# VectorE's order around a shared PSUM bank in a Winograd feed-forward kernel: the sum that frees bank b goes ahead of the residue, and two softmax steps go a place later

## The chip, the cores and the metric

The kernel runs on one core of one Trainium2 chip. The metric is the device time of one launch in microseconds (us), median of several runs. TensorE (PE in the profile, its weight loads PEld), VectorE (DVE), ScalarE (ACT), GpSimd (POOL) and SyncE (SP) each work through a queue of their own, in the order in which the program issues to them; semaphores between the queues keep the data right.

## The reference

Channel attention over four batches, then a feed-forward layer with an ELU over all tokens.

```python
B, N, C = (4, 6080, 256)            # q, k, v
n_tokens, d_model, d_ff = (24320, 256, 2048)
...
qn = q / (np.linalg.norm(q, axis=1, keepdims=True) + 1e-06)
kn = k / (np.linalg.norm(k, axis=1, keepdims=True) + 1e-06)
s = kn.transpose(0, 2, 1) @ qn / tau
s = s - s.max(-1, keepdims=True)
a = np.exp(s)
a /= a.sum(-1, keepdims=True) + 1e-09
x = (v @ a)                          # 256 channels a token
h = x @ w_in
g = np.where(h > 0.0, h, np.exp(np.minimum(h, 0.0)) - 1.0)
return g @ w_out
```

## The kernel before, in words

**Precision and folding.** Each float32 operand of a large product is split in a high part, rounded to the matmul's input format, and a low part, the residue (operand minus its high part). A product is then three matmuls: high by high, high by low, low by high. The softmaxed matrix `a` of a batch is multiplied into `w_in` once, so that a token's hidden values come straight from `v`.

**Units.** The tokens of batches 1 to 3 go through 36 chunks of 512 or 496 tokens, and each chunk through four quarters of the 2048 hidden features (`fq`). A chunk and a quarter make a unit, 144 in all (lines 1471 to 1537). Within a unit the product of a 2 by 2 block matrix with a 2 by 2 block matrix is done by Winograd's scheme, with seven block products in place of eight: A11·B11, S3·T3, S2·T2, A12·B21, S1·T1, S4·B22 and A22·T4, where the S and T are sums of blocks. Their partial sums are put together in three PSUM banks, `bank_a`, `bank_b` and `bank_e`, of which `bank_b` is one and the same for all units. `product` (line 1104) is six matmuls.

**Bank b in a unit.** ScalarE copies A11·B11 from `bank_a` into `bank_b` (line 1490) and S3·T3 from `bank_e` into `p` (`vp`, line 1492). TensorE adds S2·T2 on top in `bank_b`. VectorE then makes the sum `ve = vb + vp` (line 1500), which reads `bank_b`; only then may TensorE go on to add S1·T1 in `bank_b`. VectorE makes `vp = vb + vp` (line 1506) of that; only then may TensorE add S4·B22. So TensorE waits for VectorE at the start of S1·T1 and of S4·B22, and for ScalarE (line 1490) at the start of S2·T2.

**ELU and residues.** For each of the four blocks of hidden values ScalarE makes Relu (line 1183) and Exp (line 1184) into a buffer `held` or `other`, and VectorE combines them with the block (`largest`, line 1187). The block for row 0, half 0 is called e11 in the code, and is the first of a unit; the next is e22, then e12 and e21. Then the high part of g is made by a DMA that GpSimd issues (line 1204), for e12 by ScalarE (line 1202). The low part, g's residue, is `lo_parts` (line 1212, or two instructions of line 1210 when the row's blocks lie in `other`): it reads the block and the high part that the DMA wrote. The residue of row 0 of unit u is made in unit u+1 behind S2·T2, that of row 1 behind `largest` of e11. Row 0's blocks lie in `held[:, 0]`, which the next unit's Relu of e11 writes over, so that Relu waits until row 0's residue has been made.

**Second layer.** Between the block products stand the matmuls of the second layer, three to an item (lines 1127, 1128 and 1129, the last with g's residue as its operand), eight items a unit, two at a time (`multiply_out`). The items of row 0 of unit u begin behind S1·T1 of unit u+1.

**What sets the order.** The instructions of a unit are issued in the order of the code. Between them stand calls of `spend(engine, budget, now)`: each takes tasks from lists (loads, splits, the next batches' attention) whose inputs are far enough back, and issues them there. `now` counts quarters of a unit. A task on another engine's result is ready when that result was issued `late` places earlier; without `late`, VectorE's tasks may be issued in the same place as ScalarE's task they read (`GAP[DVE]` is 0, line 951). While units run, the attention of batches 2 and 3 is made in such tasks. The softmax part is in `plan_soft`: ScalarE takes a square root of the norms and loads the table for Exp (lines 1384 and 1386), VectorE turns this into inverse norms (lines 1391 to 1406: a guard, two halves of a reciprocal, three refining steps, again two halves of a reciprocal), scales the rows (1420 to 1422), ScalarE takes Exp with row sums (1427), VectorE inverts these sums (`over_sums`, lines 318 and 319).

Of the kernel before, what the change touches and what calls it, by code (L numbers as in the profile page):

```python
# [27 lines left out]
def in_turns(cols):  # L28

    if len(cols.shape) == 3:  # L30
        return cols.rearrange("p x (a b) -> p x b a", a=2)
    return cols.rearrange("p (a b) -> p b a", a=2)
# [22 lines left out]
def channel_attention_then_elu_ffn(ctx: ExitStack, tc, q, k, vT, tau, w_in, w_out, outT):  # L55
# [8 lines left out]
    nc = tc.nc  # L64
# [252 lines left out]
    def over_sums(sm):  # L317
        nc.vector.tensor_scalar(sm, sm, 1e-9, None, op0=ALU.add)
        nc.vector.reciprocal(sm, sm)
# [233 lines left out]
    state = {}  # L553
# [395 lines left out]
    ACT, DVE, POOL, PE, SP = "act", "dve", "pool", "pe", "sp"  # L949
# [18 lines left out]
    def task(engine, cost, fn, deps=(), when=0, level=1, late=None):  # L968

        t = Task(fn, tuple(d for d in deps if d is not None), when)  # L970
        t.late, t.engine = late, engine
        t.cost = cost
        queues[engine, level].append(t)
        return t

    def spend(engine, budget, now):
        for level in range(-2, 4):
            queue = queues[engine, level]
            while True:
                able = [t for t in (queue if level < 2 else queue[:1]) if t.ready(now)]  # L980
                if not able or able[0].cost > budget + 0.3:
                    break
                t = able[0]
                queue.remove(t)
                budget -= t.cost
                t.fn()
                t.done = now
# [30 lines left out]
    def half_of(c):  # L1018
        return span(c)[2] // 2
# [47 lines left out]
    x = s1 - 13  # L1067
# [29 lines left out]
    def product(bank, c, fq, a, t, begin=False):  # L1097
        hn = half_of(c)
        w, m = s_tiles[fq][:, :, MATRICES.index(a)], operands[c, t]
        hi, lo = (in_turns(m[:, x, 0:hn]) for x in range(2))  # L1100
        for j in range(2):
            js = slice(j * P, j * P + P)
            for k, (x, y) in enumerate(((0, hi), (0, lo), (1, hi))):
                nc.tensor.matmul(  # L1104
                    bank[:, j, 0:hn],
                    w[:, x, js],
                    y,
                    start=(begin and j == 0 and k == 0),
                    stop=(j == 1 and k == 2),
                    skip_group_check=True,  # L1110
                )
# [44 lines left out]
    def multiply_out(count, now):  # L1156
        for _ in range(count):
            if not outs:
                return
            item = outs.pop(0)  # L1160
            if item is None:
                continue
            for _ in out_matmuls(*item):
                beside(now)
# [30 lines left out]
    def exact(u, row, half, hn):  # L1195
        e = others[half] if row == 1 and u % 2 == 1 else held[:, row, half]
        return e[:, 0 : 2 * hn]
# [17 lines left out]
    def plan_chunk(c):  # L1215

        if c + 1 >= NCH:
            return
        d, t = c + 1, begins[c]
        if c == NB:  # L1220
            task(SP, 0, lambda: new_t_group(d), when=t, level=0)
        x = task(SP, 0, lambda: vraw.__setitem__(d, load_v(d)), when=t + PERIOD, level=0)
        for k in range(3):
            x = task(DVE, 0.415 if k else 0.685, lambda k=k: t_sum(d, k), [x], when=t + PERIOD, level=0)
            if k != 1:
                y = task(ACT, 0.61, lambda k=k: t_hi(d, k), [x], when=t + PERIOD, level=0, late=1)
                task(DVE, 0.685, lambda k=k: t_lo(d, k), [y], when=t + PERIOD, level=-1, late=1)
        for k, when in enumerate((2 * PERIOD, 3 * PERIOD, 3 * PERIOD + 1)):
            y = task(POOL, 0.55, lambda k=k: b_hi(d, k), when=t + when, level=0)
            task(DVE, 0.415, lambda k=k: b_lo(d, k), [y, x], level=-2, late=2)  # L1230
# [106 lines left out]
    def plan_soft(b, t):  # L1337
# [20 lines left out]
        def row_copy(ct):  # L1358
            if ct == 0:
                state[b, "a"] = work.tile([P, KT, C], F32, tag="a", bufs=1, name=f"a_{b}")  # L1360
            nc.scalar.copy(halves(state[b, "a"][:, ct]), halves_of_turns(state[b, "gram"][ct][:, 1, :]))
# [6 lines left out]
        for ct in range(KT):  # L1368
            x = task(ACT, 0.35, lambda ct=ct: row_copy(ct), [last_gram], level=0)
# [18 lines left out]
        x = task(ACT, 1.0, root, [pn], level=0)  # L1388
# [22 lines left out]
        turns = [[(0.95, lambda half=half, of=of: turned(half, of)) for half in range(2)] for of in ("ry", "y")]  # L1411
        refining = [(cost, lambda k=k: refined(k)) for k, cost in enumerate((0.42, 0.42, 0.3))]
        for cost, fn in ((0.3, guarded), *turns[0], *refining, *turns[1], (0.2, taken)):
            x = task(DVE, cost, fn, [x], level=0)

        def scaled(ct, k):
            a = state[b, "a"]
            row = halves(a[:, ct])
            (
                lambda: nc.vector.tensor_scalar(a[:, ct], a[:, ct], n["rk"][:, ct : ct + 1], None, op0=ALU.mult),  # L1420
                lambda: nc.vector.tensor_mul(row, row, n["rq"]),
                lambda: nc.vector.tensor_reduce(n["nm"][:, ct : ct + 1], a[:, ct], axis=AX.X, op=ALU.max, negate=True),
            )[k]()

        def exped(ct):
            a = state[b, "a"]
            nc.scalar.activation(
                a[:, ct], a[:, ct], AF.Exp, bias=n["nm"][:, ct : ct + 1], accum_out=state[b, "rs"][:, ct : ct + 1]
            )

        exps = []
        for ct in range(KT):
            for k, cost in enumerate((0.25, 0.42, 0.42)):
                x = task(DVE, cost, lambda ct=ct, k=k: scaled(ct, k), [x], level=0)
            exps.append(task(ACT, 0.5, lambda ct=ct: exped(ct), [x], level=0))
        sums = task(DVE, 0.2, lambda: over_sums(state[b, "rs"]), exps, level=0)

        def transposes():
            n["pt"] = ps.tile([P, KT, C], F32, tag="gram", bufs=KT, name="pt")
# [16 lines left out]
        x = task(ACT, 0.61, aT_hi, [pt, folded], level=0)  # L1456
        x = task(DVE, 0.685, aT_lo, [x], level=0)
# [13 lines left out]
    for u, (c, fq) in enumerate(units):  # L1471
        now = PERIOD * u
        b = c // NB
        hn = half_of(c)
        if fq == 0:
            plan_chunk(c)
        spend(SP, 1, now)
        assert (b, fq) in s_ready, (b, fq, u)
        e11, e12, e21, e22 = (
            exact(u, row, half, hn).rearrange("p (j t) -> p j t", j=2) for row in range(2) for half in range(2)  # L1480
        )
        vp = p7[:, :, 0:hn]
        bank_a = ps.tile([P, 2, HF], F32, tag="w", bufs=WB, name="bank_a")
        bank_e = ps.tile([P, 2, HF], F32, tag="w", bufs=WB, name="bank_e")
        va, vb, ve = (bank[:, :, 0:hn] for bank in (bank_a, bank_b, bank_e))

        product(bank_a, c, fq, "A11", "B11", True)
        if before is not None:
            before[0]()
        nc.scalar.copy(vb, va)  # L1490
        product(bank_e, c, fq, "S3", "T3", True)
        nc.scalar.copy(vp, ve)
        multiply_out(2, now)
        spend(POOL, 3.9, now)
        spend(ACT, 2.0, now)
        spend(DVE, 2.4 if u % (FQ * NB) in (0, *range(FQ * NB - FQ, FQ * NB)) else 1.7, now)
        product(bank_b, c, fq, "S2", "T2")
        if before is not None:
            before[1]()
        nc.vector.tensor_add(ve, vb, vp)  # L1500
        product(bank_a, c, fq, "A12", "B21")
        relu_exp(e11, va)
        multiply_out(2, now)
        spend(ACT, 0.7, now + 1)
        product(bank_b, c, fq, "S1", "T1")
        nc.vector.tensor_add(vp, vb, vp)  # L1506
        multiply_out(2, now + 1)
        largest(e11, va)
        hi_part(u, 0, 0, hn)
        spend(POOL, 1.2, now + 1)  # L1510
        product(bank_b, c, fq, "S4", "B22")
        product(bank_e, c, fq, "A22", "T4")
        if before is not None:
            before[2]()
        relu_exp(e22, vp)
        largest(e22, vp)
        hi_part(u, 1, 1, hn)
        relu_exp(e12, vb)
        relu_exp(e21, ve)
        largest(e12, vb)  # L1520
        hi_part(u, 0, 1, hn, True)
        multiply_out(2, now + 2)
        spend(DVE, 1.4, now + 2)
        spend(ACT, 0.4, now + 2)
        spend(POOL, 3.3, now + 2)
        spend(SP, 1, now + 2)

        def finish(e21=e21, ve=ve, u=u, hn=hn):
            largest(e21, ve)
            hi_part(u, 1, 0, hn)  # L1530

        before = (finish, lambda u=u, hn=hn: lo_parts(u, 0, hn), lambda u=u, hn=hn: lo_parts(u, 1, hn))

        for y, row in ((2, 0), (0, 1)):
            for dt in range(DT):
                for j in range(2):
                    outs.append((c, 4 * fq + y + j, ((u, row), j), dt))
# [46 lines left out]
```

## Time and profile before

| | |
|---|---|
| median of 3 runs | 2140.25 us (2137.35 to 2141.48) |
| the profiled execution's own time | 2139.17 us |
| its span, first to last instruction | 2137.4 us |
| granted TensorE clock, mean | 1.000 |
| units | 144, from about 597 us to the end |

A row of a timeline gives the start in us from the span's start, the duration, the engine, the line, the operation, what it writes and reads by the program's names, its shape and how often; in brackets the idle time of that engine just before it and what ended that. A row of a wait table gives who waited for whom, the total in us, how often, and the longest. Matmuls overlap (a new one starts before the last one's end), so an engine with a busy share of 99% may still lose time to waits.

### The profile page before, as it was taken

What the parts mean: (1) busy time and instruction counts of PE and PEld (TensorE: products, weight loads), DVE (VectorE), ACT (ScalarE), POOL (GpSimd) and SP (SyncE); (2) the same over time, 40 slices, a digit from 0 to 9 for tenths busy, and PEclk for the clock granted to TensorE, in tenths of its full rate; (3) what the DMA queues carried; (4) which work ended last, traced back from release to release, by engine and by line L of the source; (5) the groups of instructions that cost most, each with busy time, mean ns of one, the idle gap of its engine ahead of it and who ended that gap; (6) DMA issues with size and microseconds to landing.
All of it is one profiled execution on the core that took longest, in us unless ns stands there. A gap on an engine that the chain in (4) does not pass through costs nothing. (4 is left out here: it accounts for less than half of the span.)

```text
span 2137.4 us, 34932 instructions
## 1 busy us (share of the span) xinstructions
PE 2108.5 (99%) x12833; PEld 1930.5 (90%) x12833; DVE 1584.1 (74%) x2380; ACT 1485.0 (69%) x2524; POOL 439.2 (21%) x763
## 2 busy tenths in 40 slices
PE   9999999999999999999999999999999999999999
PEld 8888888899889998999899899999899999999998
DVE  7987777777777777777677777777767777776775
ACT  6877777767766776667666677667766676776765
POOL 0000000000233333321233333322133222121121
PEclk9999999999999999999999999999999999999999
DMA  9320221210357887854366778875436443333432
GB/s 361 109 79 30 72 79 64 74 56 30 133 162 215 220 221 206 224 161 133 115 188 208 201 216 217 229 202 162 130 121 188 128 124 116 113 122 111 127 99 94
DMA packets 163371, 312.27 MB, mean 146 GB/s; under 512 B 17408, under 2 KB 59520, under 8 KB 161664
## 3 DMA queue, kind: packets, MB, share of 16 engines
q0 software_dynamic: 101376, 191.00, 32.7%
q1 hardware_dynamic: 61680, 118.91, 16.2%
q8 instruction: 102, 1.67, 0.3%
q14 instruction: 69, 0.57, 0.1%
q10 hardware_dynamic: 144, 0.13, 0.0%
HBM read 134.33 MB, written 31.20 MB: 77 GB/s over the span
## 5 line engine op out<-in xcount | busy, mean ns | idle before, releaser
L1127 PE MATMUL po<-g,wo 128*128 128x512 f32 (+1 forms) x1158 | 438.9, 379 | 0.0
L1129 PE MATMUL po<-g,wo 128*128 128x512 f32 (+1 forms) x1158 | 437.1, 377 | 0.0
L1128 PE MATMUL po<-g,wo 128*128 128x512 f32 (+1 forms) x1158 | 436.9, 377 | 0.0
L1204 POOL DMA_DIRECT2D g<-held x288 | 154.1, 535 | 926.7 <-DVE held L1187 589.6
L1212 DVE TENSOR_TENSOR g<-held,g 128x1024 fp32r<-128x1024 f32 (+1 forms) x216 | 263.8, 1221 | 34.2 <-DMA g<-held 33.2
L1184 ACT ACTIVATE held<-held 128x512 f32<-128x512 f32 (+1 forms) x432 | 270.4, 626 | 13.8
L1104 PEld LDWEIGHTS bank_b<-t,s 128*128 128x128 f32 x1728 | 232.7, 191 | 48.8 <-DVE bank_e L1500 28.2
L1506 DVE TENSOR_TENSOR p<-bank_b,p 128x512 f32<-128x512 f32 (+1 forms) x144 | 98.8, 686 | 238.8 <-PE bank_b L1104 238.8
L1104 PE MATMUL bank_b<-t,s 128*128 128x256 f32 (+1 forms) x1728 | 243.2, 277 | 21.7 <-DVE bank_e L1500 15.2
L1129 PEld LDWEIGHTS po<-g,wo 128*128 128x128 f32 x1158 | 218.9, 189 | 28.3
L1104 PE MATMUL bank_e<-t,s 128*128 128x256 f32 (+1 forms) x1728 | 240.0, 275 | 0.0
L1128 PEld LDWEIGHTS po<-g,wo 128*128 128x128 f32 x1158 | 220.2, 190 | 17.2
L1127 PEld LDWEIGHTS po<-g,wo 128*128 128x128 f32 x1158 | 220.7, 191 | 13.1
L1183 ACT ACTIVATE held<-bank_a 128x512 f32<-128x512 f32 (+1 forms) x144 | 85.2, 592 | 189.6 <-PE bank_a L1104 128.9
L1104 PEld LDWEIGHTS bank_e<-t,s 128*128 128x128 f32 x1728 | 216.1, 192 | 0.0
L1104 PE MATMUL bank_a<-s,s 128*128 128x256 f32 (+1 forms) x1296 | 179.8, 275 | 0.0
L1104 PEld LDWEIGHTS bank_a<-s,s 128*128 128x128 f32 x1296 | 168.4, 192 | 4.7
L115 DVE TENSOR_TENSOR g<-e,g 128x512 fp32r<-128x512 f32 (+1 forms) x192 | 131.7, 686 | 48.6 <-ACT g L114 47.2
L114 ACT CAST g<-e 128x512 fp32r<-128x512 f32 (+1 forms) x192 | 116.7, 608 | 70.7 <-DVE e L447 38.7
L474 PE MATMUL po<-g,wo 128*128 128x512 f32 (+1 forms) x378 | 142.7, 377 | 0.0
L472 PE MATMUL po<-g,wo 128*128 128x512 f32 (+1 forms) x378 | 142.6, 377 | 0.0
L470 PE MATMUL po<-g,wo 128*128 128x512 f32 (+1 forms) x378 | 142.6, 377 | 0.0
(228 smaller groups left out, 4333.4 us busy)
## 6 DMA issues: line engine op xcount, KB each, us to landing
g<-held POOLq DMA_DIRECT2D x192, 256.0 KB, 3.0
g<-other POOLq DMA_DIRECT2D x96, 256.0 KB, 3.3
g<-held POOLq DMA_DIRECT2D x96, 248.0 KB, 2.2
acc<-sq POOLq DMA_DIRECT2D x46, 512.0 KB, 5.1
raw<-in_q_dram SPq DMA_DIRECT2D x76, 256.0 KB, 4.2
raw<-in_k_dram SPq DMA_DIRECT2D x76, 256.0 KB, 4.7
v<-in_v_dram SPq DMA_DIRECT2D x32, 512.0 KB, 5.6
out_dram<-o SPq DMA_DIRECT2D x56, 256.0 KB, 2.1
```

What stands on the lines that cost most here:

```text
L114: nc.scalar.copy(hi, src)
L115: nc.vector.tensor_sub(lo, src, hi.bitcast(F32))
L470: nc.tensor.matmul(o, wo[:, f, 0, ds], hi, start=first(c, f), stop=False)
L472: nc.tensor.matmul(o, wo[:, f, 1, ds], hi, start=False, stop=False)
L474: nc.tensor.matmul(o, wo[:, f, 0, ds], lo, start=False, stop=last(c, f))
L1104: nc.tensor.matmul(bank[:, j, 0:hn], w[:, x, js], y, start=(begin and j == 0 and k == 0), stop=(j == 1 and k == 2), skip_group_check=True,)
L1127: yield nc.tensor.matmul(o, wo[:, f, 0, ds], hi, start=begin, stop=False)
L1128: yield nc.tensor.matmul(o, wo[:, f, 1, ds], hi, start=False, stop=False)
L1129: yield nc.tensor.matmul(o, wo[:, f, 0, ds], lo, start=False, stop=end)
L1184: nc.scalar.activation(e, e, AF.Exp, scale=-1.0)
L1204: nc.gpsimd.dma_start(to, e)
L1212: nc.vector.tensor_sub(lo, held[:, row, :, 0 : 2 * hn], hi.bitcast(F32))
```

## The change

Two edits. In the unit, `before[1]()`, which is the residue of row 0 of the unit before, and the sum `ve = vb + vp` change places on VectorE: the sum is issued first. In `plan_soft`, the steps of the inverse norms and the inversion of the row sums get `late=1`: they may not be issued in the same place as ScalarE's result, but one place later; the second is also entered with a cost of 0.35 in place of 0.2.

```diff
         for cost, fn in ((0.3, guarded), *turns[0], *refining, *turns[1], (0.2, taken)):
-            x = task(DVE, cost, fn, [x], level=0)
+            x = task(DVE, cost, fn, [x], level=0, late=1)
...
-        sums = task(DVE, 0.2, lambda: over_sums(state[b, "rs"]), exps, level=0)
+        sums = task(DVE, 0.35, lambda: over_sums(state[b, "rs"]), exps, level=0, late=1)
...
         product(bank_b, c, fq, "S2", "T2")
+        nc.vector.tensor_add(ve, vb, vp)
         if before is not None:
             before[1]()
-        nc.vector.tensor_add(ve, vb, vp)
         product(bank_a, c, fq, "A12", "B21")
         relu_exp(e11, va)
```

The order of instructions changes on VectorE alone; TensorE, ScalarE, GpSimd and SyncE keep theirs. The sum is line 1500 before and line 1498 after.

VectorE in the unit in which the softmax of batch 2 begins (the 36th; batch 3 has the same rows 48 units later), before: the last steps of the unit before it, the guard and a half reciprocal, the residue of row 0, the sum, the second sum.

```order
L1187 SCALAR_TENSOR_TENSOR held<-held,bank_e 128x496
L1040 TENSOR_TENSOR t_5096<-tt_8744,t_5096 128x2x248
L1391 TENSOR_SCALAR ry<-y 128x260
L1395 RECIPROCAL ry<-ry 128x130
L1212 TENSOR_TENSOR g_5223<-held,g_5162 128x2x496
L1500 TENSOR_TENSOR bank_e<-bank_b,p_5094 128x2x248
L1506 TENSOR_TENSOR p_5094<-bank_b,p_5094 128x2x248
```

The same place after, and what follows up to the guard:

```order
L1187 SCALAR_TENSOR_TENSOR held<-held,bank_e 128x496
L1040 TENSOR_TENSOR t_5096<-tt_8744,t_5096 128x2x248
L1498 TENSOR_TENSOR bank_e<-bank_b,p_5094 128x2x248
L1212 TENSOR_TENSOR g_5224<-held,g_5162 128x2x496
L1506 TENSOR_TENSOR p_5094<-bank_b,p_5094 128x2x248
L1187 SCALAR_TENSOR_TENSOR held<-held,bank_a 128x496
L1212 TENSOR_TENSOR g_5224<-held,g_5162 128x2x496
L1187 SCALAR_TENSOR_TENSOR other_5093<-other_5093,p_5094 128x496
L1187 SCALAR_TENSOR_TENSOR held<-held,bank_b 128x496
L1062 TENSOR_TENSOR s_4777<-v_8709,s_4777 128x248
L1391 TENSOR_SCALAR ry<-y 128x260
L1395 RECIPROCAL ry<-ry 128x130
```

The sum stands ahead of the residue, here as in each of the 143 units that have a residue to make; the guard and the first half reciprocal have moved behind three blocks' `largest`. The later steps of the chain move too: the unit after this one makes one half reciprocal more, and two refining steps move from it into the one after that. From there on the chain has its old places.

VectorE at the end of the softmax, before: the last block of a unit, the inversion of the row sums (lines 318 and 319), the sums of the next chunk's T blocks, then the next unit's residue and sum.

```order
L1187 SCALAR_TENSOR_TENSOR other_5092<-other_5092,bank_e 128x496
L318 TENSOR_SCALAR sums<-sums 128x2
L319 RECIPROCAL sums<-sums 128x2
L1028 TENSOR_TENSOR tt_9266<-v_9128 128x2x248
L1029 TENSOR_TENSOR tt_9266<-tt_9266,v_9128 128x248
L1030 TENSOR_TENSOR tt_9266<-v_9128,tt_9266 128x248
L1212 TENSOR_TENSOR g_5223<-held,g_5249 128x2x496
L1500 TENSOR_TENSOR bank_e<-bank_b,p_5094 128x2x248
```

The same place after:

```order
L1187 SCALAR_TENSOR_TENSOR other_5092<-other_5092,bank_e 128x496
L1028 TENSOR_TENSOR tt_9264<-v_9128 128x2x248
L1029 TENSOR_TENSOR tt_9264<-tt_9264,v_9128 128x248
L1030 TENSOR_TENSOR tt_9264<-v_9128,tt_9264 128x248
L1498 TENSOR_TENSOR bank_e<-bank_b,p_5094 128x2x248
L1212 TENSOR_TENSOR g_5224<-held,g_5249 128x2x496
```

The inversion of the row sums has gone from there to the end of that unit, ahead of the last block's `largest`.

## The prediction

> **What bounds the kernel now.** I read the page's head first, then what TensorE and its weight loads waited for, then the timeline around one such wait.
>
> ```profile
> span 2137.4 us, 34932 instructions
> PE 2108.5 (99%) x12833; PEld 1930.5 (90%) x12833; DVE 1584.1 (74%) x2380; ACT 1485.0 (69%) x2524; POOL 439.2 (21%) x763
> ```
> ```profile
> PE bank_b L1104 <- DVE bank_e L1500: 15.2, 21, 1.7
> PE bank_b L1104 <- ACT bank_b L1490: 6.0, 6, 2.0
> ```
> ```profile
> PEld bank_b L1104 <- DVE bank_e L1500: 28.2, 33, 2.1
> PEld bank_b L1104 <- ACT bank_b L1490: 8.6, 8, 2.1
> ```
>
> TensorE bounds the kernel. What it waits for most is the sum of line 1500, which the change moves; ScalarE's copy into bank b comes second. From 1660 us on, where the attention of the later batches is done, one such wait is left. Its row in the table of that window alone, and then the timeline around it, show what a wait costs:
>
> ```profile
> PEld bank_b L1104 <- DVE bank_e L1500: 0.6, 1, 0.6
> ```
> ```profile
> 1745.64 0.83 PE L1104 MATMUL bank_b<-t,s 128*128 128x256 f32 x6
> 1748.27 0.83 PE L1104 MATMUL bank_b<-t,s 128*128 128x256 f32 x6
> ...
> 1750.24 0.83 PE L1104 MATMUL bank_b<-s,s 128*128 128x256 f32 x6
> ...
> 1755.51 0.83 PE L1104 MATMUL bank_b<-t,s 128*128 128x256 f32 x6
> 1756.59 1.23 DVE L1212 TENSOR_TENSOR g<-held,g 128x1024 fp32r<-128x1024 f32 x1 [1.31 <-DMA g<-held]
> 1757.73 0.69 DVE L1500 TENSOR_TENSOR bank_e<-bank_b,p 128x512 f32<-128x512 f32 x1
> 1758.48 0.74 PEld L1104 LDWEIGHTS bank_b<-t,s 128*128 128x128 f32 x6 [0.57 <-DVE bank_e L1500]
> 1758.48 0.94 PE L1104 MATMUL bank_b<-t,s 128*128 128x256 f32 x6 [0.17 <-DVE bank_e L1500]
> ...
> 1765.82 0.83 PE L1104 MATMUL bank_b<-t,s 128*128 128x256 f32 x6
> ```
>
> S2·T2 starts at 1745.64, 1755.51 and 1765.82: the undisturbed unit takes 9.87 us, the one with the wait 10.31. It lost 0.44, though the matmuls' row admits 0.17 and the loads' row 0.57. So a wait costs the loads' idle time less 0.13, and the 33 of them 28.2 − 33 × 0.13 = 23.9 us. That is the most that the sum's new place can bring. The Trainium skill says in Perfetto Trace Analysis, section Identifying the Most-Contended Engine, that matmul busy time is a poor measure of headroom, because matmuls are pipelined, and that the weight loads' busy share is a better one. By the matmuls' row alone the gain worked out below would be 8.7 us less, by the loads' row alone 4.3 more; the trace, with 0.44 between 0.17 and 0.57, agrees with the Trainium skill that the matmuls' row tells too little.
>
> **The sum's new place.** In the undisturbed unit S1·T1 is due at 1748.27, 1.80 after the end of S2·T2 (1745.64 + 0.83). Where nothing holds VectorE, the sum starts 0.11 after that end and takes 0.70:
>
> ```profile
> 1795.43 0.83 PE L1104 MATMUL bank_b<-t,s 128*128 128x256 f32 x6
> ...
> 1796.37 0.70 DVE L1500 TENSOR_TENSOR bank_e<-bank_b,p 128x512 f32<-128x512 f32 x1
> ```
>
> So ahead of the residue it ends about 0.8 after S2·T2, with 1.0 to spare. It waits no longer for the residue (1.14 from its start to the sum's in the stalled unit), nor for the DMA that the residue reads (1.31 there). What is still ahead of it are the tasks that `spend` puts on VectorE; they would have to run on for 0.9 past the end of S2·T2 to make TensorE wait, and apart from the units with the softmax I find none that do. One cost falls away beside that: the residue is slow where GpSimd adds at the same time, the sum isn't.
>
> ```profile
> 1049.06 0.90 POOL L830 TENSOR_TENSOR x<-x 128x256 f32<-128x256 f32 x1
> ```
> ```profile
> 1049.30 1.71 DVE L1212 TENSOR_TENSOR g<-held,g 128x992 fp32r<-128x992 f32 x1
> 1050.93 0.67 DVE L1500 TENSOR_TENSOR bank_e<-bank_b,p 128x496 f32<-128x496 f32 x1
> ```
>
> The residue still has two readers on TensorE's path: the second layer's third matmul behind S1·T1, and, in VectorE's queue, the second sum (line 1506), which frees bank b for S4·B22. An instruction of VectorE may start 0.09 before the last one's end (1756.59 + 1.23 against 1757.73), so an ordinary residue ends 0.11 + 0.70 − 0.09 + 1.23 = 1.95 after S2·T2, and S1·T1 itself ends at 1.80 + 0.83 = 2.6, so both are ready. In the four units where the adds of GpSimd or other tasks make the residue end near 3.0, I leave 0.2 to 0.4 each: 1.2 us. The first unit with a residue has no second-layer matmuls ahead of S1·T1: A12·B21 is issued within 0.66 after S2·T2 (an estimate: as long as from one product's start to the next), the sum 0.86 after it, so it keeps 0.2 + 0.27 = 0.5 (0.27 is 0.44 − 0.17).
>
> **The softmax steps.** In the unit where they begin, VectorE waited for the square root and two table loads of ScalarE ahead of the residue:
>
> ```profile
> 983.91 0.30 DVE L1391 TENSOR_SCALAR ry<-y 128x260 f32<-128x260 f32 x1 [1.25 <-ACT y L1384]
> 984.25 0.97 DVE L1395 RECIPROCAL ry<-ry 128x130 f32<-128x130 f32 x1
> 985.13 1.13 DVE L1212 TENSOR_TENSOR g<-held,g 128x992 fp32r<-128x992 f32 x1
> 986.17 0.67 DVE L1500 TENSOR_TENSOR bank_e<-bank_b,p 128x496 f32<-128x496 f32 x1
> ...
> 994.15 0.43 DVE L1400 TENSOR_TENSOR y<-y,ry 128x260 f32<-128x260 f32 x1
> 994.61 0.29 DVE L1401 TENSOR_SCALAR y<-y 128x260 f32<-128x260 f32 x1
> ...
> 1014.64 0.17 DVE L318 TENSOR_SCALAR sums<-sums 128x2 f32<-128x2 f32 x1 [0.83 <-ACT a L1427]
> ```
> ```profile
> 986.90 0.93 PE L1104 MATMUL bank_b<-t,s 128*128 128x248 f32 x6 [1.72 <-DVE bank_e L1500]
> ...
> 1018.23 0.93 PE L1104 MATMUL bank_b<-t,s 128*128 128x248 f32 x6 [1.36 <-DVE bank_e L1500]
> ```
>
> These two waits, and their twins in batch 3, stand in the 33, at 1.72 + 0.27 = 2.0 and 1.6 us. With the guard and the half reciprocal gone, the first unit's sum is free at once. The inversion of the row sums takes 0.83 of waiting and twice 0.17 of work from ahead of the second. But the moved steps reach the units between: lines 1400 and 1401, 0.72 together, now stand ahead of a sum one unit later, where the other half reciprocals stand as well. That sum starts about 1.0 after S2·T2, just in time; the residue behind it ends near 2.9, ScalarE starts that unit's Relu of e11 about 1.2 late, has a copy of the output to make before e22, and by my estimate brings its next copy into bank b 0.6 late. I leave 0.9 of the 3.6 us in each of the two batches: 1.8 us (bounds 0 and 7.2, all that these four waits cost now).
>
> **What the residue's delay costs.** The Relu of e11 writes over row 0's `held`, so it waits for the residue. S2·T2 of an ordinary unit with a copy of the output in it, and ScalarE there (its first row is e22's Relu in the unit before, which has no such copy):
>
> ```profile
> 1785.56 0.83 PE L1104 MATMUL bank_b<-t,s 128*128 128x256 f32 x6
> ```
> ```profile
> 1779.92 0.63 ACT L1183 ACTIVATE held<-p 128x512 f32<-128x512 f32 x1 [1.43 <-DVE p L1506]
> ...
> 1787.10 0.60 ACT L1183 ACTIVATE held<-bank_a 128x512 f32<-128x512 f32 x1 [0.75 <-PE bank_a L1104]
> 1787.72 0.63 ACT L1184 ACTIVATE held<-held 128x512 f32<-128x512 f32 x1
> 1788.39 0.59 ACT L1143 COPY o<-po 128x512 f32<-128x512 f32 x1
> 1789.79 0.63 ACT L1183 ACTIVATE other<-p 128x512 f32<-128x512 f32 x1 [0.81 <-DVE p L1506]
> ...
> 1794.37 0.58 ACT L1490 COPY bank_b<-bank_a 128x512 f32<-128x512 f32 x1
> ```
>
> The Relu at 1787.10 will start at about 1788.4 (S2·T2 ends at 1786.39, the residue 1.95 later). Relu, Exp and copy then end 1.9 later, at 1790.3, and e22's Relu, which started at 1789.79 after 0.81 of idle time, starts 0.4 to 0.5 late. From there to line 1490 ScalarE has no idle time, and the copy ends at 1795.35 to 1795.45 in place of 1794.95. S2·T2 is due at 1795.43 with its weights 0.2 earlier: it loses 0 to 0.26, say 0.05, once in four units from 1660 us on, some ten times: 0.5 us (at most 2.6). In a unit without that copy the idle time is 1.43 and covers the 1.3; where gram matmuls of the next batch stand between, TensorE's unit is longer and ScalarE's chain is not.
>
> The sum: 23.9 − 1.2 − 0.5 − 1.8 − 0.5 = 19.9 us. The profiled execution took 2139.17; 2139.2 − 19.9 = 2119.3. The median is 1.1 above that execution, so I forecast 2120.
>
> **The rivals.** First, ScalarE gives back more: 2.6 in place of 0.5 in the ordinary units, and the softmax units keep all of their 7.2 in place of 1.8: 2120 + 2.1 + 5.4 = 2127.5. For it speaks that its chain from e22 to line 1490 is dense; against it, that its waits come with slack elsewhere.
>
> Second, transfers take it back. The residues wait for their DMA already:
>
> ```profile
> DVE g L1212 <- DMA g<-held: 33.2, 20, 4.2
> DVE g L1210 <- DMA g<-other: 15.9, 14, 2.7
> ```
>
> The wait of row 1's residue holds up e12, ScalarE's line 1202 and 1490 behind it, and TensorE's second row of waits (8.6 in the loads). The transfers' work is the same and TensorE arrives sooner. Were that row to double, 2120 + 8.6 = 2129; were it to vanish, 2112.
>
> Third, slower: the Relu of e11 makes ScalarE the bound. Its place is line 1490 in every fourth unit (36), where the copy ends 0.5 ahead of S2·T2 (1794.95 against 1795.43). If residues ended 2.9 after S2·T2 in place of 1.95, e22's Relu would be 1.4 late there, the copy 0.9 behind its due time, and S2·T2 would lose about 0.9 with its weight loads: 36 × 0.9 = 32 us, 12 more than the gain, or 2152. It outweighs the gain from 0.56 a unit on, that is from residues that end 2.6 after S2·T2. For it speaks that this Relu waited for a residue already:
>
> ```profile
> ACT held L1183 <- DVE g L1212: 31.8, 18, 2.8
> ```
>
> against it, that only 18 units did so, and the new order adds a known 1.3 to the rest.
>
> Fourth, no change: the wait moves from S1·T1 to S4·B22, since VectorE makes the same sum, residue and sum before it. That would give 2140. Against it: S4·B22 comes 1.97 after S1·T1 (1748.27 and 1750.24 in the undisturbed unit), and the second sum needs 0.83 + 0.7 of that, so VectorE may be 0.4 late there on top of the 0.65 by which the residue ends ahead of S1·T1.
>
> **How the numbers follow.** Forecast 0.70; first rival 0.10, second 0.10, both faster; fourth 0.06; third 0.04. The range 2112 to 2131 takes in the first two, the upper end with the 1.7 us of the second part's own terms doubled on the second rival, and leaves out the last two. A measurement of this kernel tells about 0.2%, 4.3 us, from no change: faster 0.90, same 0.06, slower 0.04.
>
> **What would show it.** Right: TensorE's row for line 1498 falls from 28.2 in the loads to under 5, from 33 waits to under ten; ScalarE's wait of line 1183 for line 1212 grows to well over 100 us in total; lines 1391 and 318 no longer wait for ScalarE; the row for line 1490 stays within 5 to 15 us. The first rival would show as a row for line 1490 that grows around 1000 and 1530 us, the second as one that grows with longer waits for DMA at row 1's residue, the third as one of over 20 us spread over the units, the fourth as a new row of bank b for line 1506. A time above 2131 or below 2112 makes the sum wrong.

## The result and the profile after

The changed kernel takes 2124.76 us in the median of 4 runs (2124.21 to 2127.18), against 2140.07 of 4 runs before; the ratio is 0.9932, with a 95% interval of 0.9915 to 0.9949. It is faster, by 15 us, where 20 were forecast. The profiled execution took 2124.93 us, its span 2123.2, at a clock of 1.000. First the head of the page after, then what the matmuls and the weight loads waited for (total in us, how often, the longest).

```profile
span 2123.2 us, 35036 instructions
PE 2102.7 (99%) x12833; PEld 1932.1 (91%) x12833; DVE 1586.4 (75%) x2380; ACT 1474.8 (69%) x2524; POOL 441.5 (21%) x763
```
```profile
PE bank_b L1104 <- ACT bank_b L1490: 7.1, 9, 2.0
PE pw L800 <- DMA wi<-wi_scr: 5.9, 4, 1.8
...
PE bank_b L1104 <- DVE bank_e L1498: 0.3, 2, 0.2
```
```profile
PEld bank_b L1104 <- ACT bank_b L1490: 12.3, 14, 2.1
PEld pw L800 <- DMA wi<-wi_scr: 7.1, 4, 2.1
PEld bank_b L1104 <- DVE bank_e L1498: 1.3, 4, 0.5
```

The sum's row, 28.2 us in the loads before, is down to 1.3, and ScalarE's line 1490 is up by 3.7 (8.6 before). The second row in each fence is one that the prediction did not speak of: line 800 makes the product `pw` (the softmaxed matrix into a piece of `w_in`) and waits for a DMA that loads that piece, `wi`. Before, its row in the matmuls had been small:

```profile
PE pw L800 <- DMA wi<-wi_scr: 0.5, 1, 0.5
```

The unit that the prediction took as its example of a stall, in the timeline after, from S2·T2 on:

```profile
1741.69 0.83 PE L1104 MATMUL bank_b<-t,s 128*128 128x256 f32 x6
1742.62 0.70 DVE L1498 TENSOR_TENSOR bank_e<-bank_b,p 128x512 f32<-128x512 f32 x1 [0.96 <-PE bank_b L1104]
1743.23 1.22 DVE L1212 TENSOR_TENSOR g<-held,g 128x1024 fp32r<-128x1024 f32 x1
1744.33 0.83 PE L1104 MATMUL bank_b<-t,s 128*128 128x256 f32 x6
1744.53 0.60 ACT L1183 ACTIVATE held<-bank_a 128x512 f32<-128x512 f32 x1 [2.08 <-DVE g L1212]
```

S1·T1 starts 2.64 after S2·T2 (1744.33 against 1741.69), without a wait. The sum starts 0.10 after S2·T2's end at 1742.52 and takes 0.70, and the residue ends at 1744.45, 1.93 after it: the prediction had 0.11, 0.70 and 1.95. The Relu of e11 comes right behind the residue, at 1744.53, and ScalarE's wait for it has grown from 31.8 us to

```profile
ACT held L1183 <- DVE g L1212: 128.1, 51, 6.6
```

which costs TensorE nothing in the units of this kind. From 1660 us on, the copy of line 1490 that the prediction worked out for every fourth unit ends 0.28 us ahead of S2·T2 in most of them, where it was 0.48 before. In the traces TensorE starts 0.05 after that copy at the earliest, so 0.23 is still to spare.

To see where the difference lies, I took for every block product the time from its start to the next one's, less the shortest such time with the same matmuls between. That is what TensorE lost there. A few hundredths of a us in the shortest time, summed over 144 units, move this total by some us, so only differences between kernels are used here. Over all 144 units TensorE loses 14.1 us less than before, which is the difference of the two spans (14.2). In the stretches from A12·B21 to S4·B22, which hold the sum's wait, it loses 23.1 us less. In the stretches from S3·T3 to S2·T2, which hold the waits for line 1490 and for `wi`, it loses 8.3 more, of which 5.7 in the four units in which TensorE waits for `wi` (1.2 before, 7.0 after).

These four are the 42nd and 44th unit (counted from 0) and their twins in batch 3, the 90th and 92nd. In the 42nd and 90th a stall of the sum, one unit earlier, had hidden the wait. The 42nd before, around the load's issue by GpSimd (line 1240):

```profile
1047.48 0.74 POOL L828 TENSOR_TENSOR x<-x 128x256 f32<-128x256 f32 x1
...
1051.54 0.58 POOL L1240 DMA_DIRECT2D wi<-wi_scr  x1
...
1051.66 0.93 PE L1104 MATMUL bank_b<-t,s 128*128 128x248 f32 x6 [1.00 <-DVE bank_e L1500]
```
```profile
1057.92 0.48 PE L800 MATMUL pw<-wi,aT 128*128 128x512 f32 x1
```

And after:

```profile
1039.91 0.74 POOL L828 TENSOR_TENSOR x<-x 128x256 f32<-128x256 f32 x1
...
1042.92 0.83 PE L1104 MATMUL bank_b<-t,s 128*128 128x248 f32 x6
...
1044.02 0.58 POOL L1240 DMA_DIRECT2D wi<-wi_scr  x1
...
1050.42 0.48 PE L800 MATMUL pw<-wi,aT 128*128 128x512 f32 x1 [1.27 <-DMA wi<-wi_scr]
```

GpSimd has four additions of its own (lines 828 to 831) ahead of the issue, and needs as long for them as before: 4.06 from the first to the issue before, 4.11 after. `pw` starts 6.38 and 6.40 behind the issue. What has changed is TensorE, which before stood still ahead of S1·T1 for 1.00 + 0.27 = 1.27 and now comes that much sooner to a load that is not there. The wait removed in one unit is paid in the next: 2.7 us in these two (0.2 before, 2.9 after).

In the 44th unit no stall went away. There the residue, in its new place, falls on GpSimd's additions:

```profile
1064.34 0.75 POOL L828 TENSOR_TENSOR x<-x 128x256 f32<-128x256 f32 x1
1064.79 0.68 DVE L1498 TENSOR_TENSOR bank_e<-bank_b,p 128x496 f32<-128x496 f32 x1 [1.82 <-ACT p L1492]
...
1065.39 1.56 DVE L1212 TENSOR_TENSOR g<-held,g 128x992 fp32r<-128x992 f32 x1
1065.86 1.68 POOL L830 TENSOR_TENSOR x<-x 128x256 f32<-128x256 f32 x1
...
1068.18 0.58 POOL L1240 DMA_DIRECT2D wi<-wi_scr  x1
...
1074.47 0.48 PE L800 MATMUL pw<-wi,aT 128*128 128x512 f32 x1 [1.77 <-DMA wi<-wi_scr]
```

The same additions and the issue before:

```profile
1071.83 0.75 POOL L828 TENSOR_TENSOR x<-x 128x256 f32<-128x256 f32 x1
...
1073.35 0.74 POOL L830 TENSOR_TENSOR x<-x 128x256 f32<-128x256 f32 x1
...
1074.71 0.58 POOL L1240 DMA_DIRECT2D wi<-wi_scr  x1
```

The addition of line 830 takes 1.68 in place of 0.74, and the load is issued 3.84 after the first addition, not 2.88. `pw` then starts 6.29 after the issue, where it was 5.52 before (at 1080.23). These 0.96 and 0.77 are the 1.7 that TensorE loses more in this unit (2.0 against 0.3); in the 92nd it loses 1.3 more.

### The profile page after: what moved, and what is told of

It is laid out like the page before. It is cut to its first block, busy times and chain, and to the rows that moved or that the text cites. A ratio compares the mean times of both kernels' runs of the same rounds, so it can differ in the third digit from the quotient of the medians.

```text
span 2123.2 us, 35036 instructions
## 1 busy us (share of the span) xinstructions
PE 2102.7 (99%) x12833; PEld 1932.1 (91%) x12833; DVE 1586.4 (75%) x2380; ACT 1474.8 (69%) x2524; POOL 441.5 (21%) x763
## 5 line engine op out<-in xcount | busy, mean ns | idle before, releaser
L1127 PE MATMUL po<-g,wo 128*128 128x512 f32 (+1 forms) x1158 | 438.9, 379 | 0.0
L1129 PE MATMUL po<-g,wo 128*128 128x512 f32 (+1 forms) x1158 | 437.0, 377 | 0.0
L1128 PE MATMUL po<-g,wo 128*128 128x512 f32 (+1 forms) x1158 | 437.0, 377 | 0.0
L1104 PEld LDWEIGHTS bank_b<-t,s 128*128 128x128 f32 x1728 | 234.6, 191 | 26.6 <-ACT bank_b L1490 12.3
L1498 DVE TENSOR_TENSOR bank_e<-bank_b,p 128x512 f32<-128x512 f32 (+1 forms) x144 | 99.6, 692 | 159.1 <-PE bank_b L1104 77.9
L474 PE MATMUL po<-g,wo 128*128 128x512 f32 (+1 forms) x378 | 142.7, 377 | 0.0
L472 PE MATMUL po<-g,wo 128*128 128x512 f32 (+1 forms) x378 | 142.6, 377 | 0.0
```

The lines of the kernel that those rows point to most:

```text
L472: nc.tensor.matmul(o, wo[:, f, 1, ds], hi, start=False, stop=False)
L474: nc.tensor.matmul(o, wo[:, f, 0, ds], lo, start=False, stop=last(c, f))
L1104: nc.tensor.matmul(bank[:, j, 0:hn], w[:, x, js], y, start=(begin and j == 0 and k == 0), stop=(j == 1 and k == 2), skip_group_check=True,)
L1127: yield nc.tensor.matmul(o, wo[:, f, 0, ds], hi, start=begin, stop=False)
L1128: yield nc.tensor.matmul(o, wo[:, f, 1, ds], hi, start=False, stop=False)
L1129: yield nc.tensor.matmul(o, wo[:, f, 0, ds], lo, start=False, stop=end)
```

## The experiments

Theory: the sum's new place brought some 23 us, the softmax steps little beside it, and the missing 5 to 6 us went into the load of `wi`, which stands behind GpSimd's additions. Rivals: the softmax steps hold the difference, on one side or the other, or the delayed residue does (ScalarE's line 1490 with its Relu, row 1's residue).

The kernel before was run again beside the experiments: 2137.88 us beside e1 to e4, 2137.68 beside e5 to e8, against 2140.07 above. Each ratio is to the runs beside it, so a difference of two medians from different groups can be off by some 2 us, and the ratios are the better measure.

**The sum alone.** `e1_sum_first_alone` is the changed kernel with the softmax steps as before.

```diff
-            x = task(DVE, cost, fn, [x], level=0, late=1)
+            x = task(DVE, cost, fn, [x], level=0)
...
-        sums = task(DVE, 0.35, lambda: over_sums(state[b, "rs"]), exps, level=0, late=1)
+        sums = task(DVE, 0.2, lambda: over_sums(state[b, "rs"]), exps, level=0)
```

> The sum ahead of the residue, the softmax steps in their old places. Theory (the sum's new place is nearly the whole gain; the softmax steps only exchange one wait for another): 2126, within 3 us of the full change; TensorE waits for line 1498 about 3 us in the units near 983 and 1015 us and their twins, and loses nothing there at line 1490, where the full change loses 0.9 and 0.6. Rival (the softmax steps bring what the prediction gave them, 7.2 less 1.8): 2130.

Measured: 2126.97 us, ratio 0.9947 (0.9934 to 0.9959). The whole change has 0.9932 with an interval that overlaps, so the softmax steps on top are worth 0.15% by the two ratios, and not surely anything. The forecast of 2126 was met, and the rival's 2130 was not. What the steps still cost without the second edit, in the loads' waits from 965 to 1030 us, where batch 2's softmax lies, first in this kernel, then in the changed one:

```profile
PEld bank_b L1104 <- DVE bank_e L1498: 2.9, 3, 1.0
PEld bank_b L1104 <- ACT bank_b L1490: 1.1, 2, 0.7
```
```profile
PEld bank_b L1104 <- ACT bank_b L1490: 1.0, 1, 1.0
PEld bank_b L1104 <- DVE bank_e L1498: 0.2, 1, 0.2
```

The sum's wait in these units shrinks from 4.7 to 2.9 by its place alone, and to 0.2 with both edits. Three waits are left in e1, because in three units softmax steps still stand ahead of the sum: the guard and a half reciprocal, then lines 1399 to 1401, then the inversion of the row sums. One part of the expectation failed: TensorE does lose something at line 1490 here, 1.1 in the loads, where nothing was forecast. Over the whole kernel TensorE loses 4.3 us more in the sum's stretches than in the changed kernel; so of the 23.1 us gained there, 18.8 come by the sum's place alone.

**The softmax steps alone.** `e2_softmax_late_alone` is the kernel before with the second edit.

```diff
-        nc.vector.tensor_add(ve, vb, vp)
         if before is not None:
             before[1]()
+        nc.vector.tensor_add(ve, vb, vp)
```

(The diff is against the changed kernel.)

> The residue ahead of the sum as before, the softmax steps a place later. Theory: the waits of 1.7 and 1.4 us at the start and the end of the softmax go, but the steps now stand ahead of the residue of the two units between, whose sums then start 0.5 to 1 us late: a gain of 2 us a batch, 2136 in all, not clear of no change. Rival (the prediction's price for these steps holds by itself): 2134 or less, with no wait of over 0.5 us left between 980 and 1020 us.

Measured: 2134.71 us, ratio 0.9985 (0.9976 to 0.9994), so 3 us are gained. In the same window the sum's row in the loads falls from 4.7 in four waits to

```profile
PEld bank_b L1104 <- DVE bank_e L1500: 2.5, 3, 1.2
```

Three waits are left. In two of them (0.7 and 1.2 us) steps that moved now stand ahead of the residue and the sum; in the third (0.6) it is the sums of the next chunk's T blocks, which stood there before. The time lies between the two forecasts (2136, and 2134 or less); the rival's sign, no wait of over 0.5 us, did not come. The gain, 3 alone and 0 to 3 beside the first edit, need not add up, since both edits work on the same four waits.

**The load of `wi` ahead of GpSimd's additions.** `e3_wi_ahead` is the changed kernel with one number altered in the planner: the load's task gets a more urgent level, so GpSimd issues it before the four additions. Nothing is taken away.

```diff
-            wi = task(POOL, 0.6, load, [prior.get("pw"), *norm_deps[0:1]], level=1)
+            wi = task(POOL, 0.6, load, [prior.get("pw"), *norm_deps[0:1]], level=0)
```

> The full change, with the load of w_in's split parts (line 1240) issued by GpSimd ahead of its four adds, not behind them, in six of eight cases; nothing else moves. Theory (the matmuls of line 800 wait because the load is issued too late, and the stall of 1.2 us that used to cover it is gone): TensorE's wait for that load falls from 5.9 to under 1 us, and the time by 5 us to 2120. Rival (the transfer is slow since others share the DMA engines, whenever it is issued): the wait stays above 3 us and the time within 2 us of the full change.

Measured: 2117.86 us, ratio 0.9905 (0.9891 to 0.9918), an interval that barely touches that of the changed kernel (0.9915 to 0.9949). Of TensorE's waits for `wi` none is left, in the matmuls or the loads, so the rival (the transfer is slow whenever it is issued) fails. ScalarE's line 1490 stays:

```profile
PEld bank_b L1104 <- ACT bank_b L1490: 11.3, 14, 2.1
```

**The same on the kernel before.** `e8_wi_ahead_alone` makes e3's edit in the kernel before.

> The kernel before, with only the load of w_in's split parts ahead of GpSimd's adds. Theory (before, stalls of the sum covered that load's lateness, so its wait was 0.5 us): no change within 1.5 us, though the full change gains 6 us by the same edit. Rival (an early load helps by itself, whatever VectorE does): 4 us or more faster than before.

Measured: 2137.83 us, ratio 1.000 (0.9991 to 1.0009), so no change within 2 us. The same edit is worth 6 to 7 us with the change in place (5.8 by the ratios 0.9932 and 0.9905, 6.9 by the medians 2124.76 and 2117.86) and nothing that can be told without it. So the wait for `wi` is the change's own price: the load's place behind the additions had cost next to nothing as long as the sum stood where it was.

**Row 1's residue later.** `e4_row1_residue_later` tests the delayed residue's other side: row 1's residue, which waits for its DMA, goes behind `largest` of e12, so that e12, line 1202 and line 1490 need not wait for it.

```diff
-        if before is not None:
-            before[2]()
...
         largest(e12, vb)
+        if before is not None:
+            before[2]()
         hi_part(u, 0, 1, hn, True)
```

(Other lines between are left out.)

> The full change, with the residue of row 1 two blocks later on VectorE, behind the two steps of line 1187 for e22 and e12. Theory (at line 1490 TensorE waits because row 1's residue, held up by its DMA, holds up e12, line 1202 and line 1490): the loads' wait for line 1490 falls from 12.3 us to about 6 (what is left are the first units and the softmax ones), the time by 4 us to 2121; TensorE's third matmul of the next unit's first items may wait for the residue instead, up to 2 us in all. Rival (ScalarE itself is late, by the Relu that waits for row 0's residue): the wait for line 1490 stays at 10 to 13 us and the time where the full change is.

Measured: 2154.07 us, ratio 1.0073 (1.0059 to 1.0086): 16 us slower than the kernel before, which took 2137.88 beside it, where a gain of 4 on the changed kernel was forecast. What TensorE's loads waited for:

```profile
PEld gram L203 <- DVE qk L1318: 11.8, 16, 0.8
PEld bank_b L1104 <- DVE bank_e L1498: 11.1, 16, 1.5
PEld pw L800 <- DMA wi<-wi_scr: 10.2, 4, 3.2
...
PEld po L1129 <- DVE g L1212: 5.7, 10, 1.2
PEld bank_b L1104 <- ACT bank_b L1490: 5.0, 4, 2.1
```

Line 1490's row falls from 12.3 to 5.0. By itself that would not show the cause, since TensorE stands still elsewhere in this kernel and so comes later to line 1490. But the changed kernel's trace shows the chain directly, here in the 63rd unit: row 1's residue waits for its DMA, and e12, line 1202 and line 1490 come behind it.

```profile
1282.11 1.29 DVE L1210 TENSOR_TENSOR g<-other,g 128x512 fp32r<-128x512 f32 x2 [2.58 <-DMA g<-other]
...
1284.63 0.62 ACT L1202 CAST g<-held 128x512 fp32r<-128x512 f32 x1 [2.01 <-DVE held L1187]
...
1285.79 0.94 PE L1104 MATMUL bank_b<-t,s 128*128 128x256 f32 x6 [1.01 <-ACT bank_b L1490]
```

In e4 this wait is gone, and the four that are left are those that were named: the first two units and the two of the softmax. But the residue, 1.2 us of VectorE, now stands ahead of the tasks that VectorE does late in a unit: the low parts of the next batch's q and k (line 1318), for which the gram matmuls wait (0.9 us of TensorE's time in each of twelve units), and those ahead of the next sum. The wait of line 1129, the third matmul, is also larger than the 2 us that were allowed for it. The expectation counted the wait removed and not the queue that the instruction was moved into. Here too the wait for `wi` grows, and that is not traced further.

**How much later the residue may end.** `e5_residue_later` puts one more addition on VectorE, into a tile that nothing reads, between the sum and the residue.

```diff
         nc.vector.tensor_add(ve, vb, vp)
+        nc.vector.tensor_add(idle[:, :, 0:hn], vp, vp)
         if before is not None:
             before[1]()
```

> The full change, with one more VectorE addition into an unused tile (0.6 us from start to start) between the sum and row 0's residue in every unit: a delay of the residue alone, to 2.55 us after S2·T2. Theory (what the residue holds up is ScalarE's Relu of e11, and behind it line 1490, with slack left in most units): the units with an output copy and no gram matmuls lose 0.6 each from 1660 us on, some 7 to 12 us in all, 2135. Rival (the prediction's third: ScalarE is at its edge in every fourth unit of all 144): 0.56 and more in each of 36 units, 20 us or more, 2145 and up. Other rival (the delay has no price): within 3 us of the full change.

Measured: 2147.80 us, ratio 1.0043 (1.003 to 1.0055): 23 above the changed kernel and slower than the one before. A fourth plain unit of it, where S2·T2 starts at 1790.15 and so ends at 1790.98 (the lines are numbered one or two higher here; 1491 is 1490 of the text):

```profile
1791.70 0.68 DVE L1500 TENSOR_TENSOR idle<-p 128x512 f32<-128x512 f32 x1
...
1792.30 1.22 DVE L1212 TENSOR_TENSOR g<-held,g 128x1024 fp32r<-128x1024 f32 x1
...
1793.60 0.60 ACT L1183 ACTIVATE held<-bank_a 128x512 f32<-128x512 f32 x1 [2.66 <-DVE g L1212]
...
1800.40 0.74 PEld L1104 LDWEIGHTS bank_b<-t,s 128*128 128x128 f32 x6 [0.62 <-ACT bank_b L1491]
```
```profile
PEld bank_b L1104 <- ACT bank_b L1491: 22.5, 31, 2.2
PEld po L1129 <- DVE g L1212: 15.7, 27, 1.3
```

The residue ends at 1793.52, 2.54 after S2·T2, 0.6 later than in the changed kernel, and that turns the gain into a loss: the third rival's mechanism at work, near the point (2.6) that the prediction gave. By TensorE's lost time 12 of the 23 us lie ahead of S2·T2, 0.38 in most fourth units: the delay of 0.6 less the 0.23 that the copy of line 1490 had to spare. Another 12 lie between S1·T1 and S4·B22, where the second layer's line 1129 waits for the residue, most of it (10) in units 36 to 50 and 84 to 96, in which the next batch's attention is finished. The wait for `wi` gives 5 back, because TensorE stalls ahead of it again. In eight units the delay is more than the 0.6 that was meant: the residue, pushed back, falls on GpSimd's additions, as here in the 47th.

```profile
1120.92 1.72 DVE L1212 TENSOR_TENSOR g<-held,g 128x992 fp32r<-128x992 f32 x1
```

It takes 1.7 in each of the eight and ends 3.4 to 3.9 after S2·T2. These eight hold 6.6 of the second 12 us, so the pure price of 0.6 is smaller than 23.

**e11 in a buffer of its own.** In `e6_own_buffer` e11 of the odd units lies in a third buffer, so that no unit's Relu of e11 writes over what the residue of the unit before has still to read. The residue of such a row is two instructions in place of one.

```diff
+    third = tiny.tile([P, 2 * HF], F32, tag="early", bufs=1, name="third")
...
-        e = others[half] if row == 1 and u % 2 == 1 else held[:, row, half]
+        e = others[half] if row == 1 and u % 2 == 1 else third if row + half == 0 and u % 2 == 1 else held[:, row, half]
...
-        if row == 1 and u % 2 == 1:
+        if u % 2 == 1:
```

> The full change, with a buffer of its own for e11 in odd units, so that no Relu of e11 waits for row 0's residue any more (in odd units that residue is two instructions, 0.07 us longer together). Theory: ScalarE's wait of line 1183 for line 1212 falls from 128 us to under 30, but it was covered nearly everywhere: only the 0.9 and 0.6 us at line 1490 in the units that end the softmax go, 2123. Rival (ScalarE's late start is what took back the 5 us between forecast and result): 2119 or less, and the loads' wait for line 1490 falls from 12.3 us to under 7.

Measured: 2128.16 us, ratio 0.995 (0.9937 to 0.9964). ScalarE's wait for the residue is gone from the profile (Relu now waits for TensorE and the second sum). Neither forecast of the time came: it is not less than the changed kernel's but 3 us more, with intervals that overlap. Line 1490's row falls, though not to under 7, and time turns up at `wi` (1491 is 1490 of the text here too):

```profile
PEld pw L800 <- DMA wi<-wi_scr: 9.5, 4, 2.9
PEld bank_b L1104 <- ACT bank_b L1491: 8.9, 9, 2.1
```

So the 128 us that ScalarE waits cost TensorE about 3 in the loads (12.3 to 8.9), and what is won there is lost at the same load, whose transfer was slower in this run as well (median 7.0 us from issue to landing against 6.4). TensorE loses 4.1 us more than in the changed kernel in the four units with `wi`; why that transfer is slower is not shown. The span is 4.0 longer in this profile, of which 1.7 lie ahead of the first unit.

**Both.** `e7_wi_ahead_own_buffer` has e3's and e6's edits.

> The full change with the earlier load of w_in's split parts and with e11's own buffer in odd units: the version that should be fastest. Theory: the two gains do not touch each other, 2116 to 2117. Rival (with the loads early, ScalarE's late start becomes the next thing TensorE waits for): 2113 or less.

Measured: 2117.47 us, ratio 0.9899 (0.9885 to 0.9914), the lowest of all, but not to be told from e3. With the load ahead, nothing waits for `wi`, and line 1490's row in the loads is 7.9, the lowest of the kernels with the sum ahead, e4's and its price aside.

## Why the prediction was right, and where it was off

**The sum's new place.** Right in mechanism and nearly in size. The forecast was 23.9 − 1.2 − 0.5 = 22.2; TensorE's lost time gives 23.1, part of which (4.3, by e1) needs the second edit. The first unit with a residue kept 0.47 (0.5 forecast). Of the units with late residues only the 49th kept anything to speak of, about 0.45 in place of 1.2 for all, and there the sum itself was late: it stood behind a low part that waits for a DMA of its own. The prediction had found no such task outside the softmax.

```profile
1130.30 1.29 DVE L843 TENSOR_TENSOR s<-x,s 128x512 fp32r<-128x512 f32 x2 [1.39 <-DMA s<-x]
```

The rule that a wait costs the loads' idle time less 0.13 held: by it the rows give 23.9 before and 1.3 − 4 × 0.13 = 0.8 after, a fall of 23.1, and the starts of the matmuls give 23.1 too. The signs in the profile came as told: the row of line 1498 under 5 and under ten waits, ScalarE's wait above 100, line 1490's row between 5 and 15, no wait of lines 1391 and 318.

**The softmax steps.** The prediction misread one thing: ahead of the guard VectorE waited for one table load and the square root, which ended at 983.88, and not for two table loads; the second ran from 983.90, beside the guard. The waits, and the sum made of them, do not change by that. The rest of the working can be followed in the unit that takes lines 1400 and 1401, where S2·T2 starts at 997.47 and ends at 998.30:

```profile
999.31 0.67 DVE L1498 TENSOR_TENSOR bank_e<-bank_b,p 128x496 f32<-128x496 f32 x1
999.89 1.18 DVE L1212 TENSOR_TENSOR g<-held,g 128x992 fp32r<-128x992 f32 x1
...
1001.43 0.58 ACT L1183 ACTIVATE held<-bank_a 128x496 f32<-128x496 f32 x1 [3.18 <-DVE g L1212]
...
1008.05 0.93 PE L1104 MATMUL bank_b<-t,s 128*128 128x248 f32 x6 [0.63 <-ACT bank_b L1490]
```

The sum starts 1.01 after S2·T2 (about 1.0 forecast), the residue ends 2.77 after it (2.9), and the copy of line 1490 makes the next S2·T2 wait. This unit lost 0.9 in TensorE's time and its twin 0.6: 1.5, where 1.8 of 7.2 had been forecast to stay.

**The residue's delay.** 0.5 forecast, none found in the plain units. The copy of line 1490 came 0.2 later there, where 0.4 to 0.5 had been worked out. The mechanism behind it stood the test of e5: 0.6 us more is too much.

**The term that was missing.** The step that failed is the sum itself, "23.9 − 1.2 − 0.5 − 1.8 − 0.5 = 19.9 us". By what was measured in its terms, 23.1 − 1.5 = 21.6 us had been gained; 5.7 went to `wi` and about 1 to row 1's residues and their DMAs, which the prediction held at nothing and which vary from run to run, and with under 1 us elsewhere 14.1 are left. For `wi` there was no term. The prediction did not ask what the 33 stalls were covering, nor on whose work the residue would fall in its new place: it had noted that the residue is slow beside GpSimd's additions, and counted only VectorE's side of that. The second rival had the kind right (transfers take it back) and the transfer wrong. It looked at the residues' waits because they already had large rows in the table, 33.2 and 15.9 us; the load that took the time had 0.5. That the time lies within 2112 to 2131 is in part luck, for the upper end had been left open for row 1's residue, and another load took up the room.

**The rivals.** The first did not come about (ScalarE's row grew by 3.7 in the loads). The third's mechanism exists, as e5 shows, but only beyond the 0.23 us that the copy of line 1490 has to spare; its price there was split otherwise than forecast, half of it with the second layer's third matmul, which the prediction had counted as ready, and e5 is in part a harsher test than meant, by the eight slowed residues. The fourth is refuted: bank b never waits for line 1506.

## What to carry to other kernels

Before a stall is counted as a gain, follow the bounding engine on from it and ask of every load that it uses next when that load was issued and how much it has to spare; a row of 0.5 us in the wait table can hide a lateness as long as the stall ahead of it. A DMA that an engine issues behind its own arithmetic is late by that arithmetic: issue it first, where its buffer is free. And an instruction put ahead of another on a shared queue has a slack that can be worked out in tenths of a us from the timeline, and is best tried with a dummy instruction of known length, with a look at what else that instruction pushes aside.

## What the runs showed of the hardware

Beside VectorE's residue an addition of GpSimd took 1.68 us in place of 0.74 in the rows above; the residue took 1.56, and 1.71 in the prediction's row, in place of 1.18. Not both are slowed each time: at 1042.30 in the changed kernel the residue took 1.17, and the addition beside it 1.72. The sum, beside GpSimd's additions of lines 828 and 829, took 0.68 as it does elsewhere. The residue reads two operands in SBUF, the sum one in SBUF and one in PSUM. The Trainium skill says in SBUF — State Buffer, section Who interferes with whom, that a VectorE instruction with two SBUF inputs contends with a GpSimd instruction that reads SBUF, and one with at most one SBUF input, outside its 2-port performance modes, does not: the trace agrees in these rows. What I had not expected is where the harm landed, on a DMA that stood in GpSimd's queue behind the slowed addition.
